# One visit or two: where the cluster products of q and k stand in a fused attention and SwiGLU kernel

## The chip, the cores and the metric

The kernel runs on one core of a Trainium2 chip. The metric is the device time of one execution in microseconds. Three runs of the kernel before gave a median of 345.89 us (345.86 to 345.89).

The engines are named as the profile names them: PE multiplies matrices (PEld is its weight load), DVE is the vector engine, ACT the scalar engine, POOL the third elementwise engine, and SP only issues transfers.

## The reference

Four batches of eight heads of attention over 768 tokens with 64 channels; a query sees only the keys that have its cluster. Then a SwiGLU layer over the 3072 tokens of 512 channels.

```python
q_assign = argmax(einsum('bhsd,hcd->bhsc', q_n, c_n))     # 16 centroids per head, all normalised
k_assign = argmax(einsum('bhsd,hcd->bhsc', k_n, c_n))
mask = q_assign[:, :, :, None] == k_assign[:, :, None, :]
scores = where(mask, (q @ k.T) / sqrt(64), -1e9)
attn = softmax(scores) @ v                                # (4, 8, 768, 64)
x = attn.transpose(0, 2, 1, 3).reshape(3072, 512)
xn = x / sqrt(mean(x * x) + 1e-6) * rms_g
out = (silu(xn @ w_gate) * (xn @ w_val)) @ w_out          # d_ff = 1536
```

## The kernel before

**The mask without a mask.** Queries and keys are extended from 64 to 80 rows. The last 16 rows are the one-hot vector of the token's cluster, so that a score gets a large constant where the clusters agree, and the exponential takes that constant away again through its bias. The kernel therefore needs, for each head, the one-hot rows of q and of k.

**Groups.** Four heads make a group; there are eight, g = 0 to 7. The preparation of a group transposes q and k to channel-major (`trans`, L202: three fp32 transposes on PE into a PSUM tile `tq`, copied out by ACT), casts them to bf16 (`cast`, L220) and finds the clusters (`cluster_steps`, L255). For q (m = 0) and for k (m = 1) the cluster steps are four:

- `products` (L259, L237): for each of the four heads a product of 32 centroid columns with 384 tokens, in fp32. The four outputs lie under each other in one PSUM tile `sc`. The trace shows eight matmuls for such a tile. DVE then transposes the tile into SBUF (L244), which releases it.
- `most` (L262, L249): DVE's maximum over the 16 centroids.
- `same` (L265, L253): DVE compares with the maximum.
- `back` (L269, L271): DVE transposes the one-hot rows back.

Then `place` (L277) writes the rows into `qext` and `kext` with eight small transfers for each of q and k, issued on POOL's queue for g > 3.

**Units.** A unit is one batch and half of its queries: eight units, u = 0 to 7, each with 8 heads of 3 gaps. `attention` (L636) writes out the order of the work by hand. In each of the 24 gaps it emits two score matmuls S (L333; ACT's exponential L337 follows), in the second gap of each head also the 18 matmuls of the previous head's attention times values (`pv`, L339 on; called PV here), and then filler pieces until their planned costs reach this gap's share of the total.

**Filler.** In units 2 to 5 the filler is, in this order: the last eight pieces of the feed-forward layer of unit u - 2 (gates and values 8 to 11), the norm of unit u - 1, nine pieces of the output product of unit u - 2 (`o`), four transposes of x and the first 16 gate and value pieces of unit u - 1, and between these 16 pieces the preparation of group u + 2. The function `spread` (L509) does the interleaving: after the i-th of the 16 pieces (counting from 1) it has put in floor(n i / 16) of the n preparation pieces.

**One ring of three PSUM tiles.** All of `tq`, `sc`, `gate`, `val`, `tx` and `o` come from the pool `ps_g` with three buffers (L71), taken in turn. A new tile waits until the third tile before it has been read. A `tq` is read by ACT alone. A `gate` is read by ACT (tanh, L431) and after that by DVE (L432, called its multiply-add here); a `val` by DVE (L436); an `sc` by DVE's transpose (L244).

**Order around the change**, in units 2 to 5, as the list comes out and as the trace shows it (the numbers on gate and val count the pieces of the feed-forward layer; `tq3` is head 3 of the group; sc q and sc k are the products of q and k; DVE pieces in brackets):

```
gap 17: S | val3 | [cast k2] | [cast k2, second half] | gate4
gap 18: S | tq3 q | val4
gap 19: S PV | tq3 k | [cast k3; POOL casts, loads] | gate5
gap 20: S | [cast k3, second half] | val5 | sc q + sc k
gap 21: S | [max q] | gate6
gap 22: S PV | [compare q] | val6 | [back q] | [max k] | gate7
gap 23: S | [compare k] | val7, and then [back k], place
next unit, gap 0: S | gate8 | val8
```

In gaps 21 to 23 ACT also squares the unit's rows for the norm (L376).

Of the kernel before, what the change touches and what calls it, by code (L numbers as in the profile page):

```python
# [22 lines left out]
def kernel(  # L23
# [61 lines left out]
    def load_qk(n):  # L85
        if n < B * H:
            load(n, 0)
            load(n, 1)

    def load_v(n, vq=None):  # L90
        if n >= B * H:
            return
        stagedv[n] = stage.tile([P, ST, D], F32, tag="vs", name="vs", bufs=NV)
        (vq or nc.sync).dma_start(out=stagedv[n], in_=src(v, n))
# [107 lines left out]
    def trans(g, h, part, on=None):  # L202
        if (g, h // 2) not in qkT:
            qkT[g, h // 2] = qk32.tile([P, 2, 2, UQ], F32, tag="qkT", name="qkT")
        qk = staged[g * HG + h]
        ps = ps_g.tile([P, UQ], F32, tag="gen", name="tq")
        for i in range(HT):
            nc.tensor.transpose(ps[:, i * P:(i + 1) * P], qk[:, part, 2 * i:2 * i + 2].rearrange("p t d -> p (t d)"),  # L208
                                ident_f)
        to, by = qkT[g, h // 2][:, h % 2, part], 1.0 / ZS if part else 1.0  # L210
        if on is nc.vector:
            nc.vector.tensor_scalar_mul(to, ps, by)
        else:
            nc.scalar.activation(to, ps, ACT.Copy, scale=by)  # L214
# [5 lines left out]
    def cast(on, g, h, part, es=(0, 1)):  # L220
        for e in es:
            to = cols((kext if part else qext)[g % 4][:D, h], g, e)
            of = qkT[g, h // 2][e * D:(e + 1) * D, h % 2, part]
            if on is nc.scalar:
                nc.scalar.copy(to, of)
            else:
                on.tensor_copy(to, of)  # L227

    def vcast(n):
        nc.gpsimd.tensor_copy(vbf[n // HG % 4][:, n % HG, :, :D], stagedv[n])  # L230
# [24 lines left out]
    def cluster_steps(g, m):  # L255

        of = {}

        def products():  # L259
            of["cl"] = cluster_products(g, [(h, m) for h in range(HG)])  # L260

        def most():  # L262
            of["mx"] = largest(of["cl"])

        def same():  # L265
            of["ohT"] = asg.tile([P, UQ], BF16, tag="ohT", name="ohT", bufs=2)
            compare(of["ohT"].rearrange("p (b e c) -> p b e c", e=2, c=NC), of["cl"], of["mx"])

        def back():  # L269
            put[g, m] = asg.tile([P, UQ], BF16, tag="oh", name="oh", bufs=3)  # L270
            nc.vector.transpose(put[g, m], of["ohT"])  # L271

        return [products, most, same, back]
# [3 lines left out]
    def place(on, g, m, es=(0, 1)):  # L277

        ext = (kext if m else qext)[g % 4]
        for h in range(HG):  # L280
            for e in es:
                on.dma_start(out=ext[D:D + NC, h, e * UQ:(e + 1) * UQ],  # L282
                             in_=put[g, m][32 * h + e * NC:32 * h + (e + 1) * NC])
# [184 lines left out]
    def group_work(g):  # L468

        t, c = [], []  # L470
        for h in range(HG):
            n = g * HG + h
            t += [(0.3, lambda h=h: trans(g, h, 0)), (0.3, lambda h=h: trans(g, h, 1))]

            def others(n=n):
                vcast(n)
                load_qk(n + NQ)
                load_v(n + NV)

            def both(h=h, f=others):  # L480
                cast(nc.gpsimd, g, h, 0)
                f()
                cast(nc.vector, g, h, 1, (0,))
            if g == 2:
                c.append((0.0, others))
            else:
                c += [(0.0, both), (0.0, lambda h=h: cast(nc.vector, g, h, 1, (1,)))]
        a = []
        for m in range(2):
            a += [(0.0 if i else 0.7, f) for i, f in enumerate(cluster_steps(g, m))]  # L490
            if g == 3:
                a.append((0.0, lambda m=m: place(nc.gpsimd, g, m)))
            elif g == 2:
                a.append((0.0, (lambda: (place(nc.sync, g, 1), place(nc.sync, g, 0, (1,)))) if m else
                          (lambda: place(nc.sync, g, 0, (0,)))))
        if g > 3:
            a[:1] = [(1.4, lambda f=(a[0][1], a.pop(4)[1]): [x() for x in f])]
            a.append((0.0, lambda: [place(nc.gpsimd, g, m) for m in range(2)]))
        return t, c, a

# [4 lines left out]
    def group(g):  # L505
        t, c, a = group_work(g)
        return [x for h in range(HG) for x in t[2 * h:2 * h + 2] + c[2 * h:2 * h + 2]] + a
# [149 lines left out]
    for u in range(1, NU):  # L657
        ffn, o, g = ffn_work(u - 1), out_work(u - 2) if u > 1 else [], u + 2
        if u == 1:
            t, c, a = group_work(2)  # L660
            t3, c3, a3 = group_work(3)
            n = LEAD - 4
            o3 = [(0.0, lambda i=i: load_o(i)) for i in range(0, FC, 4)]
            prep = c + a + spread(weave(t3[n:], c3), o3) + a3[:5]
            idle = const.tile([P, 1], BF16)

            def norm():
                rms(0)
                nc.gpsimd.tensor_copy(idle, xn[0][:, HT - 1, DM - 1:])
                for h in range(HG):  # L670
                    casts(pool_, H + h, K0, Q0, K1, Q1)

            hooks = {(1, 0, 0): late[6], (1, 0, 1): lambda: (late[7](), norm())}
            hooks.update({(1, *divmod(2 + i, HT)): t3[i][1] for i in range(n)})
            hooks[1, *divmod(LEAD - 1, HT)] = lambda: xtrans_all(0)
            fill = spread(ffn[CC:CUT], prep)
            attention([(1, h) for h in range(H)], fill, LEAD, hooks)
        else:
            fill = ffn_work(u - 2)[CUT:] + [(0.0, lambda u=u: rms(u - 1))]
            fill += border(spread(o[:3], [(0.0, f) for _, f in a3[5:]]) + o[3:], ffn) if u == 2 else border(o, ffn)  # L680
            attention([(u, h) for h in range(H)], fill + spread(ffn[CC:CUT], group(g) if g < NG else []))
# [41 lines left out]
```

## Time and profile before

| what | value |
|---|---|
| median of three runs | 345.89 us |
| the profiled execution | 345.89 us, of which the span is 344.1 us |
| PE busy in the span | 336.9 us (98%) |
| ACT, DVE, POOL busy | 261.1, 221.7, 112.7 us (76%, 64%, 33%) |
| the `sc` matmuls of L241 | 96, 486 ns each in the median |
| DVE's transposes L244, maxima L249, compares L253, transposes L271 | 12 each; 569, 524, 552, 575 ns |
| DVE's multiply-adds L432 and L436 | 550 and 552 ns |
| PE's clock | full in units 2 to 5 |

The 1.8 us beside the span lie before and after what the profiler records; the change does not touch them. Two views matter. The chain of waits follows the work that ended last backwards, from each instruction to what released it; on PE its pieces are streaming times (four matmuls of a gate take 0.65 us there). The timeline lists instructions by their own start and duration, and there the same four take 0.81 us, because the last one's run through the array is included. A start in the timeline is therefore about 0.16 us ahead of the same piece's start in the chain where PE runs without a wait (gate6 of unit 3 starts at 144.13 us in the one and at 144.29 us in the other).

### The profile page before, as it was taken

The page shows a single profiled execution, that of the slowest core. Times are in us where ns is not written, and L with a number is a line of the kernel's source. Part 1 is how long each engine was busy: PE and PEld are TensorE (multiplying, and loading weights), DVE is VectorE, ACT ScalarE, POOL GpSimd, SP SyncE. Part 2 cuts the span into 40 slices and gives each one's busy share as a digit, 9 for nine tenths or more (in the row PEclk, how much of TensorE's full clock was granted, in tenths as well). Part 3 has the DMA queues.
Part 4 walks back from the last instruction along what each step waited for, and adds up shares of the span by engine and source line. Part 5 has one row for each costly group of instructions (what it writes and reads, how often), then busy time and mean ns, then how long its engine had stood idle before and what let it go on. Part 6 is the DMA issues. An engine that isn't in the chain of part 4 may idle for free.

```text
span 344.1 us, 8007 instructions
## 1 busy us (share of the span) xinstructions
PE 336.9 (98%) x3045; PEld 208.3 (61%) x3045; DVE 221.7 (64%) x540; ACT 261.1 (76%) x449; POOL 112.7 (33%) x225
## 2 busy tenths in 40 slices
PE   8999999999999999999999999999999999999996
PEld 4547657655766567665665656756566656655654
DVE  6999796984588636795467845686455645575330
ACT  5899979857879878787787878988688887764322
POOL 6999596234335304271131801427000000000000
DMA  8999979873450114401130010000100011001002
GB/s 273 362 226 214 260 161 235 139 248 115 129 177 14 44 56 145 139 17 40 61 94 2 22 57 38 2 3 22 63 32 0 3 41 53 2 1 64 30 2 91
DMA packets 27302, 31.62 MB, mean 92 GB/s; under 512 B 4480, under 2 KB 24320, under 8 KB 27264
## 3 DMA queue, kind: packets, MB, share of 16 engines
q1 hardware_dynamic: 18608, 25.02, 22.3%
q0 software_dynamic: 8368, 5.71, 10.3%
q8 instruction: 24, 0.39, 0.5%
q10 hardware_dynamic: 288, 0.39, 0.4%
q14 instruction: 14, 0.11, 0.1%
HBM read 28.35 MB, written 6.29 MB: 101 GB/s over the span
## 4 chain that ended last, share of the span: by engine, by line
PE 82%; DVE 9%; ACT 6%; issue 2%; DVEq 0%; POOL 0%; ACTq 0%; POOLq 0%
PE o L448 17%; PE gate L423 16%; PE val L423 16%; PE s L333 15%; PE acc L351 9%; ACT pT L337 4%; PE tq L208 3%; PE sc L241 3%; DVE th L432 2%; PE tx L396 1%; DVE gvT L436 1%; ACT th L431 1%; PE warm L117 1%; DVE pads L312 1%; DVE kext L317 1%
## 5 line engine op out<-in xcount | busy, mean ns | idle before, releaser
L337 ACT ACTIVATE pT<-s,off 128x768 bf16<-128x768 f32 x192 | 171.7, 905 | 38.5 <-PE s L333 37.2
L333 PE MATMUL s<-qext,kext 80*128 80x384 bf16 x384 | 94.8, 327 | 1.6 <-ACT pT L337 0.8
L423 PE MATMUL gate<-xnT,wg 128*128 128x384 bf16 x384 | 78.5, 325 | 0.5
L423 PE MATMUL val<-xnT,wv 128*128 128x384 bf16 x384 | 78.1, 325 | 0.2
L432 DVE SCALAR_TENSOR_TENSOR th<-th,gate 128x384 f32<-128x384 f32 x84 | 46.2, 550 | 44.7 <-ACT th L431 43.2
L448 PE MATMUL o<-wo,gvT 128*128 128x512 bf16 x276 | 67.4, 379 | 0.0
L227 POOL CAST qext<-qkT 64x384 bf16<-64x384 f32 x64 | 35.3, 557 | 74.9 <-ACT qkT L214 67.2
L333 PEld LDWEIGHTS <-kext 80*128 80x128 bf16 x384 | 36.3, 98 | 32.7 <-issue 8.1
L436 DVE SCALAR_TENSOR_TENSOR gvT<-th,val 128x384 bf16<-128x384 f32 x84 | 46.4, 552 | 8.1 <-PE val L423 3.6
L423 PEld LDWEIGHTS <-wg 128*128 128x128 bf16 x384 | 36.5, 97 | 24.1 <-issue 2.1
L423 PEld LDWEIGHTS <-wv 128*128 128x128 bf16 x384 | 36.5, 97 | 23.6 <-issue 1.5
L431 ACT ACTIVATE th<-gate 128x384 f32<-128x384 f32 x84 | 41.4, 492 | 10.9 <-PE gate L423 9.9
L351 PEld LDWEIGHTS <-pT 128*128 128x128 bf16 x1152 | 43.4, 97 | 10.1 <-DVE x L358 1.1
L351 PE MATMUL acc<-vbf,pT 128*128 128x65 bf16 x1152 | 45.6, 193 | 0.6 <-ACT pT L337 0.2
L448 PEld LDWEIGHTS <-gvT 128*128 128x128 bf16 x276 | 25.5, 97 | 25.3 <-issue 0.6
L208 PE MATMUL tq<-ident_f,qk 128*128 128x128 f32 x192 | 31.2, 280 | 0.0
L282 POOL DMA_DIRECT2D qext<-oh x40 | 19.1, 487 | 33.6 <-DVE oh L271 33.6
L214 ACT ACTIVATE qkT<-tq 128x384 f32<-128x384 f32 x57 | 26.8, 492 | 2.7 <-PE tq L208 2.2
L397 DVE TENSOR_SCALAR xnT<-tx,gcol 128x384 bf16<-128x384 bf16 x28 | 10.4, 413 | 26.9 <-PE tx L396 26.9
L208 PEld LDWEIGHTS tq<-ident_f,qk 128*128 128x128 f32 x192 | 22.9, 143 | 6.4 <-ACT qkT L214 1.0
L451 ACT COPY o_sb<-o 128x512 f32<-128x512 f32 x23 | 13.5, 586 | 15.2 <-PE o L448 15.2
L282 POOL DMA_DIRECT2D kext<-oh x40 | 19.1, 485 | 8.4 <-DVE inv L356 8.4
(81 smaller groups left out, 247.5 us busy)
## 6 DMA issues: line engine op xcount, KB each, us to landing
qk<-in_q_dram SPq DMA_DIRECT2D x32, 192.0 KB, 3.8
vs<-in_v_dram SPq DMA_DIRECT2D x32, 192.0 KB, 4.2
out_dram<-o_sb SPq DMA_DIRECT2D x23, 256.0 KB, 2.0
qk<-in_k_dram SPq DMA_DIRECT2D x30, 192.0 KB, 4.0
wg<-in_moe_w_gate_dram POOLq DMA_DIRECT2D x4, 384.0 KB, 9.2
wv<-in_moe_w_val_dram POOLq DMA_DIRECT2D x4, 384.0 KB, 11.3
wo<-in_moe_w_out_dram POOLq DMA_DIRECT2D x3, 512.0 KB, 8.3
qext<-oh POOLq DMA_DIRECT2D x40, 12.0 KB, 1.6
```

The source lines that it names most:

```text
L208: nc.tensor.transpose(ps[:, i * P:(i + 1) * P], qk[:, part, 2 * i:2 * i + 2].rearrange("p t d -> p (t d)"), ident_f)
L214: nc.scalar.activation(to, ps, ACT.Copy, scale=by)
L227: on.tensor_copy(to, of)
L282: on.dma_start(out=ext[D:D + NC, h, e * UQ:(e + 1) * UQ], in_=put[g, m][32 * h + e * NC:32 * h + (e + 1) * NC])
L333: nc.tensor.matmul(ps[:, j, :w] if nt == HT else flat[:, j * w:(j + 1) * w], lhsT=cols(kext[g % 4][:KR, hh], g, kc // HT, kc % HT * P, (kc ...
L337: nc.scalar.activation(pT[u, h][:, n * i:n * i + n, :w], of, ACT.Exp, bias=off, scale=scale * ZS)
L351: nc.tensor.matmul(acc[:, h % 2, t], lhsT=pT[u, h][:, kc, t * P:(t + 1) * P], rhs=vbf[g % 4][:, hh, kc % HT * 2 + kc // HT], start=kc == 0 ...
L423: nc.tensor.matmul(ps, lhsT=w[:, c, f * P:(f + 1) * P], rhs=xnT[u][:, c, :n], start=c == 0, stop=c == CC - 1)
L431: nc.scalar.activation(th, ps, ACT.Tanh, scale=0.5)
L432: nc.vector.scalar_tensor_tensor(th, th, 1.0, ps, op0=ALU.add, op1=ALU.mult)
L436: nc.vector.scalar_tensor_tensor(gvT[u][:, f, :n], gates[u], 0.5, ps, op0=ALU.mult, op1=ALU.mult)
L448: nc.tensor.matmul(outs[u], lhsT=gvT[u][:, f, t * P:(t + 1) * P], rhs=wo[:, f], start=f == 0, stop=f == FC - 1)
```

## The change

```diff
         if g > 3:
-            a[:1] = [(1.4, lambda f=(a[0][1], a.pop(4)[1]): [x() for x in f])]
             a.append((0.0, lambda: [place(nc.gpsimd, g, m) for m in range(2)]))
```

`a` is the list of the group's cluster pieces. The removed line took the products of k (piece 4) out of their place and put them into piece 0, right behind the products of q, with a planned cost of 1.4. Without it the products of q and of k are two pieces of 0.7 each, and the products of k stand after the `back` of q. This holds for groups 4 to 7, which are prepared in units 2 to 5.

The list of preparation pieces grows from 24 to 25, so `spread` puts in floor(25 i / 16) after the i-th piece in place of floor(24 i / 16). The two differ from i = 9 (gate4) on: 14 in place of 13 there. The order of the units' pieces up to gate4 stays, and from there it is:

```
gap 17: S | val3 | [cast k2] | [cast k2, second half] | gate4
gap 18: S | tq3 q | tq3 k | val4
gap 19: S PV | [cast k3; POOL casts, loads] | gate5
gap 20: S | [cast k3, second half] | sc q | val5
gap 21: S | [max q] | gate6 | [compare q] | [back q] | val6
gap 22: S PV | sc k | gate7
gap 23: S | [max k] | [compare k] | val7, and then [back k], place
next unit, gap 0: S | gate8 | val8
```

No instruction is added or taken away.

## The prediction

> **What bounds the kernel now.** I read the page first, then the chain of waits through unit 3 (about 109 to 150 us; the other three units with the removed line look the same to a few hundredths), and last the timeline of the gaps that change. The page:
>
> ```profile
> span 344.1 us, 8007 instructions
> PE 336.9 (98%) x3045; PEld 208.3 (61%) x3045; DVE 221.7 (64%) x540; ACT 261.1 (76%) x449; POOL 112.7 (33%) x225
> PE 82%; DVE 9%; ACT 6%; issue 2%; DVEq 0%; POOL 0%; ACTq 0%; POOLq 0%
> ```
>
> The chain runs on PE for 82% of the span, so in units 2 to 5 each microsecond of PE work or of PE standing still is a microsecond of the end. The chain, one visit to the products in group 3 first (k and q apart there already), then unit 3:
>
> ```profile
> 47.48 0.78 PE sc L241 x8
> 48.26 0.44 PE s L333 x2
> ...
> 142.44 1.43 PE sc L241 x16
> 143.86 0.43 PE s L333 x2
> ...
> 148.66 0.47 DVE th L432
> 149.13 0.04 issue
> 149.18 0.81 PE val L423 x4
> ```
>
> See here what a visit costs (0.78 us for one tile, 1.43 us for two, and 0.43 to 0.44 us for the scores behind it where they take 0.33 elsewhere), and the one place where the products make PE wait: val8 waits for DVE's multiply-add of gate7, its third tile back. The timeline of gap 14, where two `tq` already stand side by side, and then of gaps 17 to 19:
>
> ```profile
> 131.64 0.90 PE L208 MATMUL tq<-ident_f,qk 128*128 128x128 f32 x6
> 132.35 0.55 DVE L436 SCALAR_TENSOR_TENSOR gvT<-th,val 128x384 bf16<-128x384 f32 x1
> 132.37 0.49 PE L333 MATMUL s<-qext,kext 80*128 80x384 bf16 x2
> 132.96 0.81 PE L423 MATMUL gate<-xnT,wg 128*128 128x384 bf16 x4
> ...
> 137.45 0.81 PE L423 MATMUL gate<-xnT,wg 128*128 128x384 bf16 x4
> 138.12 0.71 DVE L227 CAST kext<-qkT 64x384 bf16<-64x384 f32 x2
> 138.30 0.49 ACT L431 ACTIVATE th<-gate 128x384 f32<-128x384 f32 x1 [0.29 <-PE gate L423]
> 138.43 0.49 PE L208 MATMUL tq<-ident_f,qk 128*128 128x128 f32 x3
> 138.76 0.81 PE L423 MATMUL val<-xnT,wv 128*128 128x384 bf16 x4
> 138.87 0.56 DVE L432 SCALAR_TENSOR_TENSOR th<-th,gate 128x384 f32<-128x384 f32 x1
> 140.28 0.52 PE L208 MATMUL tq<-ident_f,qk 128*128 128x128 f32 x3
> 140.64 0.81 PE L423 MATMUL gate<-xnT,wg 128*128 128x384 bf16 x4
> ```
>
> Lines 5 to 10 are gate4, its tanh and multiply-add, tq3 q and val4. Gate4 is not fully read until 139.43. Before the change that holds nobody up.
>
> **The change part by part.** All sums are for one unit, from this one execution; it took 345.89 us, which is also the median.
>
> *tq3 k moves in front of val4.* The three transposes and the ACT copy are the same work. Two `tq` side by side take 0.73 us (131.64 to 132.37) where apart they take 0.33 (138.43 to 138.76) and 0.36 (140.28 to 140.64): +0.04. The larger part is the ring. Val4's third tile back was val3; with tq3 k between them it is gate4. Val4 could start at 138.43 + 0.73 = 139.16, but gate4's multiply-add ends at 139.43, and a matmul follows its releaser by about 0.05 (132.90 to 132.96): it starts at 139.48. That is a wait of 0.32. Check: val4 starts 139.48 in place of 138.76, 0.72 later, and 0.36 of transposes are gone from gap 19: 0.36 = 0.32 + 0.04. The bounds: nothing, if DVE came to gate4 earlier; 0.26 as for gate2 in gap 14, which could have followed the scores of 132.37 by 0.33, at 132.70, and started at 132.96; 0.39, if two `tq` took only 0.66. I take 0.32, from the rows of the very instructions, none of which moves ahead of that point. Behind val4 on PE's queue stands everything; ACT and DVE have nothing that would catch up, and the next tiles are ready: gate5 needs tq3 q (read at 139.97), sc q needs tq3 k, which ACT reads right behind it.
>
> *Two visits in place of one.* PE: 2 x 0.78 - 1.43 = +0.13. Behind each visit the next matmuls cost 0.10 more (scores 0.43 against 0.33); that is now paid twice, +0.10. Sum +0.23. Behind the visits now stand val5 and gate7, full-height matmuls, for which the nearest row is the output product behind the visit of unit 2: eight of them took 1.83 against 1.73 elsewhere, also 0.10. From below, 0.13, if they hide it; from above 0.23, as I know no row that shows more. The Trainium skill, TensorEngine Tiling (Array Packing), section Key Properties, speaks against the change: switching the tiling mode, not just the tile, drains the array. If each switch cost the 0.16 us by which four matmuls' duration in the timeline exceeds their streaming time, a second visit with its two switches would cost 0.32 and the unit's sum would be 0.09 higher; the sum does not use it. The rows show no loss on the way in: group 3's visit starts at 47.48, where the gate in front of it, which began at 46.83, ends its 0.65.
>
> *val8's wait goes.* Gate8 runs from 148.43 to 149.08 in the chain; val8 would end at 149.73 and ends at 149.18 + 0.81 = 149.99: 0.26. After the change DVE reaches gate7 behind sc k's transpose, with 0.6 us to spare (worked out next): -0.26. From below, 0: if gate7 stays late.
>
> *What is late next: val7.* Its third tile back becomes val6, and compare q and back q now stand before val6's multiply on DVE. Count from the end of gap 21's scores in the chain (144.29 before). Gate6's multiply-add starts at 146.21, so +1.92, since its tanh waits on ACT behind an exponential (144.39) and the squares (145.19); both follow the scores as before. DVE starts these half-microsecond instructions 0.46 to 0.50 apart, so val6's multiply starts at 1.92 + 0.47 + 0.47 + 0.50 = 3.36 and ends at 3.91, seen at 3.96. PE has gate6 0.65, val6 0.65, scores 0.33, PV 0.55, sc k 0.78 + 0.10, gate7 0.65, scores 0.33 = 4.04, in timeline starts 3.88. So val7 waits 0.08. Gate7's multiply-add follows sc k's transpose and ends near 4.9, where val8 needs it at 5.6. From above: `back` carries several semaphore waits, seen from 147.31 to 147.65 in the chain, where they lie under the running multiply; if compare q does not cover them, 0.34 more, 0.42 in all. From below 0.
>
> *At nothing:* the same 4 transposes, 2 maxima, 2 compares of DVE. POOL's 16 transfers per unit (about 0.49 us each to issue) stay behind `back`; those of unit 3 are out at 156.1, and group 5 is first read in gap 12 of unit 4, near 169. Head 3's three loads on SP and POOL's casts stay in gap 19, 0.36 later; the loads fetch rows of the group after next, two units (82 us) ahead.
>
> *Sum:* 0.36 + 0.23 - 0.26 + 0.08 = +0.41 per unit, four units +1.64 us: 345.89 + 1.64 = 347.5 us, 0.5% slower.
>
> **The rivals.** A measurement tells 0.2%, 0.69 us, from no change.
>
> *A, not slower: gate4 is read in time.* One mechanism, in gap 18: if its multiply-add ended 0.32 earlier, val4 would not wait. For it: DVE is busy just before with two casts of head 2 (0.71 us from 138.12); were they elsewhere, only the tanh (to 138.79) would bound it. Against it: even then 138.82 + 0.56 is 139.38, so ACT alone holds it up. Sum 0.41 - 0.32 = +0.09, 346.25 us: no change to be told. It decides from 0.24 us of the wait gone (0.17 per unit is the bound).
>
> *B, more: val7 becomes the long wait.* `back` does not hide its semaphores, 0.34 more per unit: +0.75, 348.9 us. For it: the same piece shows in the chain of waits in three of the four units. Against it: the multiply that it followed is as long as the compare that it now follows.
>
> *C, faster: the products were only in the way.* The wait of val8 goes, the second visit hides behind loads, and val4's release is not on the ring as I read it: -0.26 per unit, 344.9 us. For it: only that bubble. Against it: the rows of both visits and the ring's rule, which the waits of gate2 and val8 bear out.
>
> **How the numbers follow.** My forecast 0.66, A 0.12, B 0.16, C 0.06. The forecast's own range is 346.7 to 348.2: 0.20 to 0.58 a unit, from gap 14's 0.26 for the wait with 0.13 for the visits to 0.39 with a val7 wait of 0.2. The range for 8 in 10 goes down to A and up to B: 346.2 to 348.9. Slower by over 0.2%: the forecast and B without a bit of the forecast's low end, 0.80; within 0.2%: A and that bit, 0.13; faster 0.07.
>
> **What would show it.** After: val4 behind six `tq` starts about 0.05 us after the multiply-add of gate4 ends, and appears so in the chain; two blocks of eight `sc` of 0.78; no wait of val8; val7 close behind DVE's multiply of val6. Units of 41.1 us become 41.5. I am wrong if val4 follows the transposes with no wait (A), if val7 starts over 0.3 us late (B), or if a unit becomes shorter (C).

## The result and the profile after

The changed kernel takes 348.28 us in the median of four runs (347.92 to 348.38) where the kernel before takes 345.89 (345.86 to 346.1): a ratio of 1.0066 with an interval of 1.0048 to 1.0083, slower by 1.7 to 2.9 us. The forecast was 347.5 us, 0.5% slower. The profiled execution of the changed kernel took 348.26 us.

Its page, the lines that answer to those shown of before:

```profile
span 346.5 us, 8001 instructions
PE 338.8 (98%) x3045; PEld 208.4 (60%) x3045; DVE 221.3 (64%) x540; ACT 261.1 (75%) x449; POOL 112.8 (33%) x225
PE 85%; DVE 8%; ACT 5%; issue 1%; POOL 0%; ACTq 0%; DVEq 0%; POOLq 0%
```

The same number of instructions on each of these engines, the same busy time on ACT, 0.4 us less on DVE, and 2.4 us more of span. Such a change is read from where PE stands. The timeline of gaps 17 and 18 in unit 3 after the change (start, duration, engine, what; of a timeline, here and below, only the rows that the text reads are shown):

```profile
138.23 0.81 PE L423 MATMUL gate<-xnT,wg 128*128 128x384 bf16 x4
139.08 0.49 ACT L431 ACTIVATE th<-gate 128x384 f32<-128x384 f32 x1 [0.29 <-PE gate L423]
139.21 0.82 PE L208 MATMUL tq<-ident_f,qk 128*128 128x128 f32 x6
139.65 0.55 DVE L432 SCALAR_TENSOR_TENSOR th<-th,gate 128x384 f32<-128x384 f32 x1
140.25 0.81 PE L423 MATMUL val<-xnT,wv 128*128 128x384 bf16 x4 [0.23 <-DVE th L432]
```

Head 3's transposes of q and of k stand side by side as six, and val4 starts 0.05 us after gate4's multiply-add ends (139.65 + 0.55 = 140.20). The view of waits in units 2 to 5 lists this wait once per unit, and the kernel before has no such row. (The view counts PE as idle only when the last run through the array is over. Val8 in the kernel before starts 0.09 us after that, at 149.18 behind 148.27 + 0.82, which the view does not list; its wait shows in the chain alone.)

```profile
PE val L423 <- DVE th L432: 0.9, 4, 0.2
```

The chain of waits through gaps 20 to 23 of unit 3 after the change:

```profile
142.91 0.78 PE sc L241 x8
143.70 0.76 PE val L423 x4
...
146.96 0.78 PE sc L241 x8
147.74 0.76 PE gate L423 x4
...
148.83 0.80 PE val L423 x4
...
150.61 0.65 PE val L423 x4
```

Two visits of 0.78 us, and behind each a gate or val of 0.76 where 0.65 is usual. Val7 has 0.80: it waited 0.15. The last line is val8, which now streams in 0.65 with no wait.

**Where the time went, unit by unit.** The clean measure is how much later the same score matmuls start than in the kernel before. The first scores of unit 2 are 0.22 us later (65.17 against 64.94), those of gap 3 of unit 6 are 2.38 later, and in between, counted at gap 3, each unit adds 0.50 to 0.55: 2.16 us in four units, 0.54 a unit. After that nothing is added. The 0.2 at the start is not the change's: it is there at the very first scores (10.61 against 10.37), before anything that the change moves. Over the profiled executions of this study these first scores start anywhere from 9.99 to 10.89 us. The table below therefore gives the shift per unit, from the first scores of unit 2 to the scores of gap 3 in unit 6, each from one profiled execution, beside the medians.

### The profile page after: what moved, and what is told of

Read it like the earlier page. It is cut to its first block, busy times and chain, and to the rows that moved or that the text cites. A ratio compares the mean times of both kernels' runs of the same rounds, so it can differ in the third digit from the quotient of the medians.

```text
span 346.5 us, 8001 instructions
## 1 busy us (share of the span) xinstructions
PE 338.8 (98%) x3045; PEld 208.4 (60%) x3045; DVE 221.3 (64%) x540; ACT 261.1 (75%) x449; POOL 112.8 (33%) x225
## 4 chain that ended last, share of the span: by engine, by line
PE 85%; DVE 8%; ACT 5%; issue 1%; POOL 0%; ACTq 0%; DVEq 0%; POOLq 0%
PE o L448 17%; PE val L423 17%; PE gate L423 17%; PE s L333 15%; PE acc L351 9%; ACT pT L337 3%; PE tq L208 3%; PE sc L241 3%; DVE th L432 1%; PE tx L396 1%; DVE gvT L436 1%; DVE kext L227 1%; PE warm L117 1%; DVE pads L312 1%; DVE kext L317 1%
```

## The experiments

All of them are measured beside the kernel before on one chip. Each edit moves pieces within the interleaved list of units 2 to 5, with one helper:

```diff
+    def moved(w, x, behind):
+        w.remove(x)
+        w.insert(w.index(behind) + 1, x)
...
-            attention([(u, h) for h in range(H)], fill + spread(ffn[CC:CUT], group(g) if g < NG else []))
+            own = group(g) if g < NG else []
+            w = spread(ffn[CC:CUT], own)
+            if own:
+                moved(w, ..., ...)
+            attention([(u, h) for h in range(H)], fill + w)
```

`own` is the list of preparation pieces (own[13] is tq3 k, own[18] compare q, own[19] back q); ffn[4 + 2 f] is gate f and ffn[5 + 2 f] val f.

The theory under test: the loss is a sum of three terms and a gain on PE's path, namely the reordering in gap 18 (0.36 a unit), the second visit (0.23), val7's wait and the loss of val8's wait. The rival: the second visit is what costs, and the reordering is harmless.

| kernel | base | median, us | kernel before beside it | ratio (interval) | shift per unit, us |
|---|---|---|---|---|---|
| the change | | 348.28 | 345.89 | 1.0066 (1.0048 to 1.0083) | +0.54 |
| tq3 k back behind val4 | changed | 346.79 | 346.06 | 1.0021 (1.0012 to 1.0029) | +0.18 |
| tq3 k ahead of val4, alone | before | 347.27 | 346.06 | 1.0036 (1.0024 to 1.0048) | +0.36 |
| back q behind val6 | changed | 347.65 | 346.06 | 1.0044 (1.0032 to 1.0056) | +0.39 |
| back q directly behind compare q | before | 346.47 | 346.06 | 1.0010 (1.0002 to 1.0019) | +0.11 |
| two visits without the waits | changed | 346.00 | 346.15 | 0.9998 (0.9989 to 1.0007) | +0.03 |
| back q and max k behind gate7 | before | 347.03 | 346.15 | 1.0028 (1.0019 to 1.0037) | +0.23 |
| cast k0, second half, behind val1 | before | 345.93 | 346.15 | 0.9993 (0.9984 to 1.0002) | -0.05 |
| both of these two | before | 346.86 | 346.15 | 1.0021 (1.0011 to 1.0030) | +0.18 |
| compare q and max k ahead of gate6 | before | 345.37 | 345.94 | 0.9984 (0.9975 to 0.9993) | -0.19 |
| cast behind val1, tq1 k's copy on DVE | before | 345.06 | 345.94 | 0.9972 (0.9961 to 0.9982) | -0.27 |
| both of these two | before | 344.39 | 345.94 | 0.9954 (0.9940 to 0.9967) | -0.44 |

### The reordering undone, and alone

```diff
# on the changed kernel
+                moved(w, own[13], ffn[13])    # tq3 k behind val4
```

> The changed kernel with one swap: tq3 k goes back behind val4, so the products still make two visits but the order of gaps 18 and 19 is that of before. Ring theory (val4 waits for gate4's multiply-add because the list grew by one): 0.36 us a unit comes back, four units 1.44, so about 346.6 us, 0.7 above the kernel before. Rival (the second visit to the products is what costs): nothing comes back, about 348.2 us.

```diff
# on the kernel before
+                moved(w, own[13], own[12])    # tq3 k behind tq3 q, ahead of val4
```

> The kernel before with the same swap the other way: tq3 k stands in front of val4, and the products keep their one visit. Ring theory: +0.36 us a unit, +1.44 in all, 347.3 us, with val4 starting 0.05 us after gate4's multiply-add. Rival (the second visit is what costs): no change, 345.9 us.

The first came to 346.79 us, 0.73 above the kernel before, the second to 347.27, 1.21 above it. The timeline of gap 18 in unit 3, the first kernel and then the second:

```profile
139.14 0.49 PE L208 MATMUL tq<-ident_f,qk 128*128 128x128 f32 x3
139.47 0.81 PE L423 MATMUL val<-xnT,wv 128*128 128x384 bf16 x4
139.58 0.55 DVE L432 SCALAR_TENSOR_TENSOR th<-th,gate 128x384 f32<-128x384 f32 x1
```

```profile
138.54 0.82 PE L208 MATMUL tq<-ident_f,qk 128*128 128x128 f32 x6
138.98 0.55 DVE L432 SCALAR_TENSOR_TENSOR th<-th,gate 128x384 f32<-128x384 f32 x1
139.58 0.81 PE L423 MATMUL val<-xnT,wv 128*128 128x384 bf16 x4 [0.23 <-DVE th L432]
```

With three transposes in front of it, val4 starts before gate4's multiply-add has even begun; with six, it starts 0.05 behind its end. The shifts are 0.18 and 0.36 a unit, and their sum is the whole change's 0.54. Two thirds of the loss therefore have nothing to do with the cluster products: they come from the list being one piece longer, which moves tq3 k across val4. The rival, that the second visit is what costs, would have left the first kernel at 348.2 us and the second at no change. It falls.

### Val7's wait

```diff
# on the changed kernel
+                moved(w, own[19], ffn[17])    # back q behind val6
```

> The changed kernel with back q behind val6 in the list, so that on DVE val6's multiply follows compare q at once. Theory (val7's wait of 0.15 us comes from back q ahead of val6's multiply): val7 starts without a wait, -0.15 a unit, -0.6 in all, about 347.7 us. Rival (val7 is held by something else, the tanh of gate6 on ACT): no change, 348.3 us.

```diff
# on the kernel before
+                moved(w, own[19], own[18])    # back q directly behind compare q
```

> The kernel before with back q directly behind compare q, in front of val6's multiply. Theory (an instruction of DVE that reads its predecessor's result starts 0.59 us after it in place of 0.47): everything behind is 0.12 us later on DVE, val8's wait grows by about that, +0.1 a unit, +0.4 to +0.5 in all, 346.3 us. Rival (the 0.59 belongs to back q's waits for semaphores, which it has in every place): no change, 345.9 us.

The first gains 0.15 a unit (0.39 where the change has 0.54) and comes to 347.65 us; the second loses 0.11 and comes to 346.47. DVE in gaps 22 and 23 of unit 3, in the changed kernel and then with back q behind val6, each with the start of val7 as its last line. In the first, val7 follows val6's multiply by 0.05 us (148.25 + 0.52 = 148.77); in the second the multiply has been over for 0.48 us (147.73 + 0.55 = 148.28):

```profile
147.16 0.55 DVE L253 TENSOR_TENSOR ohT<-scT,mx 128x384 bf16<-128x384 f32 x1
147.75 0.58 DVE L271 STREAM_TRANSPOSE oh<-ohT 128x384 bf16<-128x384 bf16 x1
148.25 0.52 DVE L436 SCALAR_TENSOR_TENSOR gvT<-th,val 128x384 bf16<-128x384 f32 x1
148.82 0.81 PE L423 MATMUL val<-xnT,wv 128*128 128x384 bf16 x4
```

```profile
147.27 0.55 DVE L253 TENSOR_TENSOR ohT<-scT,mx 128x384 bf16<-128x384 f32 x1
147.73 0.55 DVE L436 SCALAR_TENSOR_TENSOR gvT<-th,val 128x384 bf16<-128x384 f32 x1
148.23 0.58 DVE L271 STREAM_TRANSPOSE oh<-ohT 128x384 bf16<-128x384 bf16 x1
148.76 0.81 PE L423 MATMUL val<-xnT,wv 128*128 128x384 bf16 x4
```

In the first, back q starts 0.59 us after compare q, whose result it reads, that is 0.04 after its end. In the second, the multiply that reads nothing of compare q starts 0.46 after it, before it has ended, and back q, behind a multiply that it does not read, starts 0.50 after that one, 0.05 before its end. The kernel before with back q put right behind compare q shows the same, and what it does to val8, the last line:

```profile
146.42 0.55 DVE L253 TENSOR_TENSOR ohT<-scT,mx 128x384 bf16<-128x384 f32 x1
147.01 0.58 DVE L271 STREAM_TRANSPOSE oh<-ohT 128x384 bf16<-128x384 bf16 x1
...
148.41 0.54 DVE L432 SCALAR_TENSOR_TENSOR th<-th,gate 128x384 f32<-128x384 f32 x1
...
149.00 0.81 PE L423 MATMUL val<-xnT,wv 128*128 128x384 bf16 x4
```

Again 0.59. Is it the dependence, or back q's own waits for semaphores? In the trace of the changed kernel the sequencer's records of those waits lie in unit 3 from 146.71 to 147.05, and compare q itself starts only at 147.16, so they are over before it. In unit 2, where the trace has two of them in place of four, back q stands just as far behind: it starts at 106.11 behind a compare that ran from 105.52 to 106.07. A compare behind the maximum that it reads shows it as well (107.98 + 0.53, and it starts at 108.55). Over the thirteen profiles, in the preparation of groups 4 to 7, every back directly behind its compare (12) and every compare directly behind its maximum (32) starts 0.03 to 0.04 us after the end, and every back behind a multiply that it does not read (92) 0.04 to 0.09 before it. So it goes with reading the predecessor's result. The Trainium skill, VectorE: DVE Perf Modes, section The DRAIN you can't avoid, says that the next instruction does not start until the pipe has emptied, and that one that is not held back starts earlier. The rows here show both kinds, 0.04 us behind the end and up to 0.09 ahead of it.

### The second visit by itself

```diff
# on the changed kernel
+                moved(w, own[13], ffn[13])    # tq3 k behind val4
+                moved(w, own[19], ffn[17])    # back q behind val6
```

> The changed kernel with tq3 k back behind val4 and back q behind val6: two visits, with neither of the waits that the change brought and without val8's wait. Theory (a second visit costs 0.23 us by itself, val8's wait was 0.22): 0.0 against the kernel before, 345.9 us, and 0.9 above the kernel before without val8's wait. Rival (a second visit costs only its 0.13 of streaming): 345.5 us. Rival (the drains of the array cost 0.32): 346.3 us.

346.00 us where the kernel before has 346.15: no difference. The chain of waits in gaps 20 to 23 and the next gap, unit 3:

```profile
141.61 0.78 PE sc L241 x8
142.39 0.76 PE val L423 x4
...
145.66 0.78 PE sc L241 x8
146.44 0.76 PE gate L423 x4
...
147.52 0.65 PE val L423 x4
...
149.15 0.65 PE val L423 x4
```

No wait is left, neither at val7 (147.52) nor at val8 (149.15). Against the kernel before, the scores of gap 23 start 0.24 to 0.25 later in each unit, which is the price of the second visit (in the chain 0.13 inside the visits and 0.11 behind them), and 0.21 to 0.25 of this is given back in gap 0, where val8 waits no more: +0.03 a unit. Of the three prices on record, 0.23 holds; 0.13 would have shown as -0.10 a unit and 0.32 as +0.10. (The medians alone tell these apart only just: their interval is -0.4 to +0.2 us for four units.)

The prediction read from the chain that nothing is lost on the way into a visit. The timeline shows a loss there too. After the change, gap 20 of unit 3:

```profile
142.43 0.49 PE L333 MATMUL s<-qext,kext 80*128 80x384 bf16 x2
...
142.84 0.85 PE L241 MATMUL sc<-qkT,cblk 128*32 128x384 f32 x8
```

The visit starts 0.41 us behind scores that other work follows 0.33 behind them; the visit of the kernel before starts 0.75 behind the start of a val (141.62 to 142.37) where 0.65 is usual. So 0.08 to 0.10 of the price is lost on the way in, and the rest between the visit's first product and the work behind it. The chain hides this because it starts a piece where the piece in front ends. The section Key Properties of the Trainium skill's TensorEngine Tiling (Array Packing) has the array drain at every switch of the tiling mode. That agrees with a loss on both sides of a visit; whether the drain is what costs was not tested.

### A wait that moves: two attempts on the kernel before

The bubble at val8 (0.21 to 0.26 a unit) and the one at gate2 in gap 15 (0.26) are in the kernel before. Both looked as if one piece moved back on DVE would free them.

```diff
# val8: on the kernel before
+                moved(w, own[19], ffn[18])    # back q behind gate7
+                moved(w, own[20], own[19])    # max k behind it
```

> The kernel before with back q and the maximum of k moved behind gate7 in the list, so that DVE reads gate7 about 0.9 us earlier. Theory: val8's wait of 0.21 to 0.26 us a unit goes, -0.9 in all, 345.0 us. Rival (another wait takes its place at once, gate9 on val7's multiply): no change, 345.9 us.

```diff
# gate2: on the kernel before
+                moved(w, own[3], ffn[7])      # second half of head 0's cast of k behind val1
```

> The kernel before with the second half of head 0's cast of k behind val1 in the list, so that DVE reads val1 about 0.37 us earlier. Theory: gate2, which waits for that in gap 15, starts 0.26 us earlier in each of four units, -1.05 in all, 344.85 us. Rival (the wait moves to the next tile, tq1 k or val2): no change, 345.9 us.

```diff
# both: the three lines above
```

> The kernel before with both moves of the two runs before this one. Theory (two separate waits of the ring, each on PE's path): the gains add, -1.95 in all, 343.95 us. Rival (one of them hides the other): no better than 344.9 us.

None did what the theory expected. The first is 0.88 us slower than the kernel before, the second gains 0.05 a unit, which its times (345.93, interval 0.9984 to 1.0002) do not tell from nothing, and both together are 0.71 slower. The times of the second and the third fit their rivals, but the waits that came in place are other ones than the rivals named. In the first, val8's wait does go (gap 1 starts 0.21 to 0.25 earlier), and then 0.30 is lost in gap 1 and, in three of the four units, 0.19 in gap 2. Its timeline around the first of these:

```profile
148.44 0.55 DVE L432 SCALAR_TENSOR_TENSOR th<-th,gate 128x384 f32<-128x384 f32 x1 [0.19 <-ACT th L431]
...
149.41 0.51 DVE L249 TENSOR_REDUCE mx<-scT 128x24 f32<-128x384 f32 x1
149.95 0.56 DVE L253 TENSOR_TENSOR ohT<-scT,mx 128x384 bf16<-128x384 f32 x1
...
151.39 0.51 DVE L432 SCALAR_TENSOR_TENSOR th<-th,gate 128x384 f32<-128x384 f32 x1
...
151.95 0.81 PE L423 MATMUL val<-xnT,wv 128*128 128x384 bf16 x4
```

Gate7's multiply-add came so early that it waited 0.19 for its tanh with DVE idle, the maximum and the compare that reads it now stand back to back, and so gate8's multiply-add (151.39) is late for val9 (151.95). DVE had no slack in this stretch, and the move put work back in it.

In the second, gate2 starts without a wait (0.25 gained), but tq2 k then waits for val2:

```profile
134.58 0.51 ACT L431 ACTIVATE th<-gate 128x384 f32<-128x384 f32 x1
...
135.12 0.55 DVE L432 SCALAR_TENSOR_TENSOR th<-th,gate 128x384 f32<-128x384 f32 x1 [1.72 <-ACT th L431]
...
135.86 0.54 DVE L436 SCALAR_TENSOR_TENSOR gvT<-th,val 128x384 bf16<-128x384 f32 x1
...
136.45 0.55 PE L208 MATMUL tq<-ident_f,qk 128*128 128x128 f32 x3
```

DVE stood idle for 1.72 us until the tanh of gate2 came from ACT, which ran two copies of `tq1` and an exponential before it; so val2 was read only at 136.40, tq2 k (the last line) started 0.05 behind that, and 0.20 of the 0.25 was lost again.

### The same bubbles, with the work put where the engine stands idle

What the two failures point to: DVE idles 1.26 us ahead of gate6's multiply-add and 1.72 ahead of gate2's (1.80 in the kernel before), each time for a tanh.

```diff
# on the kernel before: compare q and max k ahead of gate6
+                moved(w, own[18], own[17])
+                moved(w, own[20], own[18])
```

> The kernel before with compare q and the maximum of k moved in front of gate6 in the list: on DVE they then run in the 1.26 us in which it waits for the tanh of gate6, and not between the reads of gate6, val6 and gate7. Theory (val8's wait is DVE work that stands ahead of gate7's multiply-add in a stretch without slack; the earlier move behind gate7 only pushed it onto gate8): val8's wait of 0.21 to 0.26 us goes and val9 does not wait either, -0.21 a unit, about -0.85 in all, 345.3 us where the kernel before has 346.15. Rival (DVE has no slack anywhere from gap 21 to gap 1 of the next unit, so any move comes back as a wait): no change or slower.

```diff
# on the kernel before: tq1 k copied out by DVE, and the cast behind val1
-            t += [..., (0.3, lambda h=h: trans(g, h, 1))]
+            t += [..., (0.3, lambda h=h: trans(g, h, 1, nc.vector if g > 3 and h == 1 else None))]
...
+                moved(w, own[3], ffn[7])
```

> The kernel before with the second half of head 0's cast of k behind val1 (as in the run that gained 0.05 us a unit) and with the copy of tq1 k on DVE in place of ACT. Theory (gate2's wait came back as tq2 k's wait on val2, because DVE stood idle 1.7 us for the tanh of gate2, which stood on ACT behind the two copies of tq1): with one copy less on ACT the tanh is 0.4 us earlier and neither waits, -0.25 a unit, about -1.0 in all, 345.15 us. Rival (ACT's queue is held by the exponentials, not by the copies): -0.05 a unit as before, 345.95 us.

```diff
# both edits
```

> Both of the edits of the two runs before this one. Theory (two separate places): the gains add, -1.85 in all, 344.3 us. Rival (no slack on DVE): no better than the better of the two.

All three came out near their expectations: 345.37, 345.06 and 344.39 us where the kernel before has 345.94, and -0.19, -0.27 and -0.44 a unit. DVE in gaps 21 to 23 of unit 3 with the first edit, and val8:

```profile
145.03 0.56 DVE L253 TENSOR_TENSOR ohT<-scT,mx 128x384 bf16<-128x384 f32 x1
145.50 0.54 DVE L249 TENSOR_REDUCE mx<-scT 128x24 f32<-128x384 f32 x1
146.25 0.56 DVE L432 SCALAR_TENSOR_TENSOR th<-th,gate 128x384 f32<-128x384 f32 x1 [0.21 <-ACT th L431]
...
148.23 0.52 DVE L432 SCALAR_TENSOR_TENSOR th<-th,gate 128x384 f32<-128x384 f32 x1
...
148.96 0.81 PE L423 MATMUL val<-xnT,wv 128*128 128x384 bf16 x4
```

The idle time ahead of gate6's multiply-add is 0.21 in place of 1.26, and gate7's (148.23) is done 0.21 before val8 starts. With the second edit the tanh of gate2 starts in gap 15 behind one copy and one exponential:

```profile
133.82 0.50 ACT L431 ACTIVATE th<-gate 128x384 f32<-128x384 f32 x1
134.35 0.56 DVE L432 SCALAR_TENSOR_TENSOR th<-th,gate 128x384 f32<-128x384 f32 x1 [0.87 <-ACT th L431]
...
135.09 0.54 DVE L436 SCALAR_TENSOR_TENSOR gvT<-th,val 128x384 bf16<-128x384 f32 x1
...
135.92 0.49 PE L208 MATMUL tq<-ident_f,qk 128*128 128x128 f32 x3
```

Val2 is read at 135.63, ahead of tq2 k at 135.92, and the gain of 0.25 stays. The last kernel, with one visit to the products, beats both kernels of this case: 0.9954 of the kernel before, interval 0.9940 to 0.9967.

## Why the prediction was right

The direction, the places and the mechanism of each term were right; the sum was 0.41 a unit where 0.54 was measured. The 348.28 us lie just above the forecast's own range (346.7 to 348.2) and inside that for 8 in 10 (346.2 to 348.9).

- *tq3 k moves in front of val4, +0.36.* Measured alone, 0.36. Val4 followed gate4's multiply-add by 0.05 as said; the time between the start of tq3 q and that of val4 is 1.04 us (139.21 to 140.25), predicted 1.05. Rival A, in which gate4 is read in time, did not happen.
- *Two visits, +0.23.* Measured 0.24 to 0.25. The reading that nothing is lost on the way in was wrong (0.08 to 0.10 is), but the sum took the price from rows of whole visits, in which that loss is contained. The output product behind the visit of unit 2 was the right row for the gate and the val that now stand behind.
- *val8's wait goes, -0.26.* It went. But 0.26 is unit 3's figure; in units 2, 4 and 5 the scores behind it gain 0.21 to 0.22. I took the unit that I had open for all four, and it was the one with the largest wait: some 0.15 us too much over four units.
- *val7 waits, +0.08.* It waits 0.15. The step that was mis-sized is the spacing on DVE: I counted 0.47 from compare q to back q, from rows in which neighbours do not read each other's results. Back q reads what compare q wrote, and starts 0.59 after it. Val6's multiply then took 0.52 in place of 0.55, so that 0.07 a unit is left, nearly 0.3 us. Rival B had this place right and named another cause, semaphores that are not hidden; the excess was a fifth of what B asked, and it came with the dependence.
- *At nothing.* The transfers, the loads and POOL's casts show no wait of PE in the view of waits after. Nothing is lost or gained from gap 3 of unit 6 on: the shift stays 2.38.
- *The start.* 0.24 us of the profiled difference lies before the first scores and belongs to no step of mine. The medians of the experiments agree with four times their shifts to within 0.3 us without it, but, by the spread of those first scores, a single pair of executions of this kernel can't be compared to better than some 0.5 us unless it is aligned behind the start.

Per unit the four terms are 0.36 + 0.24 + 0.15 - 0.21 = 0.54, as measured.

## What to carry to other kernels

In an order written out by proportion, adding or removing one piece shifts all pieces behind it; count what crosses what, and which buffer of a short ring each tile then gets, before costing the edit itself. Here a wait on the path was freed by moving work into a stretch in which the engine in question stood idle; where the work was merely moved behind the instruction that released the wait, it came back as the next wait. Check with a shift table by stage, aligned behind the start, where each part of a small difference arises.

## What the hardware showed that was not expected

A back behind its compare, or a compare behind its maximum, each reading its predecessor's result, started 0.03 to 0.04 us after that one's end; the same instructions behind one that they do not read started up to 0.09 before the end. In a stretch without slack that 0.12 us is seen in the time. The gap is not the same for every pair: a val's multiply directly behind the multiply-add of its own gate starts 0.10 after the end (after the change 151.62 + 0.52, then 152.24). And reading the predecessor is not the only thing that holds an instruction back: the cast of a head's second half starts 0.04 after the end of a multiply-add of which it reads nothing (before the change 131.38 + 0.55, then 131.97). What holds it was not tested.

The first scores of the kernel started between 9.99 and 10.89 us in the profiled executions although nothing ahead of them differed; in the slower ones the transposes and products of the first heads start later, and what they wait for there was not tested.
